# The opening of a convolution-and-expansion kernel rebuilt: taps spread by PE, bands from bf16 products, idle matmuls, w_in in column halves, unit 0 ahead of tile 0, channels regrouped in the cast

## Chip, cores, metric

One core of a Trainium2 chip. The metric is the device time of one execution in microseconds (us), the median of several; lower is better. All runs quoted are of state fast. Spans and points in time come from the profiled execution of each kernel, which is some 1.8 us shorter than its device time.

## The reference

```python
# x: 8 x 4096 x 192 fp32; weight: 8 heads x 7 taps; w_in 192 x 2048; w_out 2048 x 192
w = softmax(weight, axis=-1)                    # per head
conv[b, s, head, :] = sum_k w[head, k] * x[b, s + k - 6, head, :]     # zeros before s = 0
h = conv.reshape(32768, 192) @ w_in
out = (h * cos(h)) @ w_out                      # 32768 x 192, fp32
```

## The kernel before

Tokens come in units of 1024 and tiles of 512. The convolution is a matmul: a band matrix per head (`band`, 128 x 256, bf16), built on the chip from the softmaxed taps, is multiplied by x in bf16. The result is copied to SBUF (`ct`), turned by a DMA transpose into `cT`, and tile after tile goes through the expansion (`h`, L264), the cosine on ACT, the product `g` on DVE (L274) and the second matmul (`o_ps`, L290). The steady loop isn't touched by the change; the opening is. Cut to that:

```python
w_bc = consts.tile([128, H, K], FP32)           # taps, to all partitions by one DMA
nc.scalar.dma_start(out=w_bc, in_=bass.AP(... ap=[[0, 128], [K, H], [1, K]]))
load_unit(0, 0, NB)                             # first half of unit 0
w_src = moe_w_in.rearrange("(h k r) (t f) -> k t h r f", h=H, r=R, t=2)
for k in range(NC):                             # w_in: 6 loads
    for t in range(2):
        nc.sync.dma_start(out=w_f[64 * t : 64 * t + 64, k, :, :]..., in_=w_src[k, t])
load_unit(0, NB, UB); load_unit(1)
...                                             # softmax: 5 DVE steps and one exp -> wn
prod = consts.tile([128, H, E, K], FP32)
strip = consts.tile([128, H, E], FP32)
for eng, hs in ((nc.vector, slice(0, 4)), (nc.gpsimd, slice(4, 8))):
    eng.tensor_tensor(out=prod[:, hs], in0=mask..., in1=wn[:, hs]..., op=ALU.mult)
    nc.vector.tensor_reduce(out=strip[:, hs], in_=prod[:, hs], ..., op=ALU.add)
    for q in range(4):
        eng.tensor_copy(out=band[32 * q : 32 * q + 32, hs, 32 * q : 32 * q + E], in_=strip[...])
...
def cast_unit(u, n0=0, n1=UB):
    copy = nc.scalar.copy if u == 0 and n0 == 0 else nc.gpsimd.tensor_copy
    ...
    copy(out=bf[u][:, n0 + 1 : n1 + 1, :], in_=x_tiles[u][:, n0:n1, :])
...                                             # first half of unit 0 convolved and transposed by PE
nc.gpsimd.tensor_copy(out=w[:, 0], in_=w_f[:, 0])
nc.vector.tensor_copy(out=w[:, 1], in_=w_f[:, 1])
nc.scalar.copy(out=w[:, 2], in_=w_f[:, 2])
...
# h: an expansion step; a, b: second half of unit 0; c, d: convolution of unit 1 (tile 0) or later ones;
# m8: 8 steps of the second matmul; s: cosine and product; ea...: copies of a convolution
PE_ORDER = "h0 c1 m8 c2 h1 m8 h2 h3 m16 | h4 h5 m8 h6 m12 h7 m12"
ACT_ORDER = "P s0 ec s1 s2 s3 Q s4 s5 s6 s7"
PE_FIRST = "h0 a1 h1 a2 b1 h2 b2 h3 | h4 h5 d1 h6 d2 c1 h7 c2 x"      # tile 0
ACT_FIRST = "s0 s1 ea s2 eb s3 s4 s5 s6 ed s7 ec"
```

## Time and profile before

| | kernel before |
|---|---|
| device time, median of 4 | 755.99 us (755.06 to 756.5) |
| profiled span | 753.7 us |
| PE busy | 724.6 us, 96% |
| start of the first `g` on DVE | 22.24 us |
| start of tile 1's first expansion step | 34.36 us |
| start of tile 2's first expansion step | 52.08 us |
| from there to the end | 701.6 us |

Once PE is saturated, a change of the opening moves everything after by a constant, so I mark three points and the stretches between them.

### The profile page before, as it was taken

To read this page: it belongs to the slowest core of one execution; us is meant where nothing else is said; L and a number is where in the kernel's file an instruction comes from. 1 tells how busy PE (TensorE), PEld (TensorE's weight loads), DVE (VectorE), ACT (ScalarE), POOL (GpSimd) and SP (SyncE) were. 2 spreads that over 40 slices of the span, in tenths; PEclk is the share of its full clock that TensorE was granted. 3 is DMA by queue.
4 is the path that set the end of the run, shared out by engine and by line. 5 is a ranking of instruction groups with operands and counts; after the bars stand their busy time and mean duration, and the time that the engine had idled before them with its cause. 6 is when DMAs were issued, how large, how long until landed. Compare 5 with 4: busy or idle time off the path is not lost.

```text
span 753.7 us, 26680 instructions
## 1 busy us (share of the span) xinstructions
PE 724.6 (96%) x12060; PEld 646.8 (86%) x12060; DVE 616.5 (82%) x533; ACT 624.4 (83%) x778; POOL 110.0 (15%) x112
## 2 busy tenths in 40 slices
PE   1699999999999999999999999999999999999997
PEld 1378999999999999999999999999999999999876
DVE  5658888888888888888888888888888888888893
ACT  3668888888888888888888888888888888888883
POOL 4310111110111110011111011111101111101000
PEclk9989999999999999999999999999999999999999
DMA  7434334334535424433432442442454543243301
GB/s 203 113 86 127 85 108 127 94 99 127 116 77 127 127 77 116 127 90 103 128 105 88 127 120 73 127 127 74 119 128 89 104 127 107 86 128 85 82 27 64
DMA packets 167633, 79.99 MB, mean 106 GB/s; under 512 B 99552, under 2 KB 167136, under 8 KB 167520
## 3 DMA queue, kind: packets, MB, share of 16 engines
q1 hardware_dynamic: 167376, 78.26, 39.1%
q8 instruction: 94, 1.54, 0.8%
q14 instruction: 19, 0.16, 0.1%
q10 hardware_dynamic: 144, 0.03, 0.0%
HBM read 28.34 MB, written 25.17 MB: 71 GB/s over the span
## 4 chain that ended last, share of the span: by engine, by line
PE 95%; POOL 1%; issue 1%; DVE 1%; ACT 1%; DMA 1%; POOLq 0%; SPq 0%
PE h L264 46%; PE o_ps L290 45%; PE h L168 3%; DMA w_bc<-in_weight_dram 1%; POOL x_bf L157 0%; POOL wo L360 0%; DVE strip L123 0%; DVE band L125 0%; ACT o_sb L302 0%; ACT cs L270 0%; DVE prod L121 0%; POOL band L125 0%; ACT w L250 0%; POOL ct L218 0%; ACT ct L182 0%
## 5 line engine op out<-in xcount | busy, mean ns | idle before, releaser
L274 DVE TENSOR_TENSOR g<-h,cs 128x1024 bf16<-128x1024 f32 x512 | 605.5, 1221 | 115.8 <-ACT cs L270 108.9
L270 ACT ACTIVATE cs<-h 128x1024 bf16<-128x1024 f32 x512 | 511.4, 1025 | 78.9 <-PE h L264 74.3
L290 PE MATMUL o_ps<-wo,g 64*128 64x192 bf16 x8192 | 452.5, 243 | 1.2 <-ACT o_sb L302 1.2
L290 PEld LDWEIGHTS <-g 64*128 64x128 bf16 x8192 | 419.8, 94 | 35.8 <-SPq L138 1.8
L264 PE MATMUL h<-cT,w 64*128 64x512 bf16 x3072 | 439.1, 379 | 2.9 <-ACT ct L182 1.3
L264 PEld LDWEIGHTS <-w 64*128 64x128 bf16 x3072 | 234.1, 94 | 37.9 <-issue 4.1
L218 POOL COPY ct<-ct 128x1536 bf16<-128x1536 bf16 (+1 forms) x32 | 46.4, 1449 | 580.9 <-ACT ct L182 580.9
L168 PE MATMUL h<-x_bf,band 64*128 64x192 bf16 (+2 forms) x784 | 74.7, 247 | 19.7 <-DVE band L125 11.4
L168 PEld LDWEIGHTS <-band 64*128 64x128 bf16 (+1 forms) x784 | 56.2, 96 | 27.6 <-DVE band L125 11.4
L182 ACT CAST ct<-h 128x384 bf16<-128x384 f32 (+1 forms) x128 | 54.4, 477 | 23.9 <-PE h L168 19.2
L302 ACT COPY o_sb<-o_ps 128x384 f32<-128x384 f32 x128 | 61.3, 479 | 10.1 <-PE o_ps L290 8.2
L157 POOL CAST x_bf<-x_f 128x1536 bf16<-128x1536 f32 (+1 forms) x32 | 46.3, 1448 | 3.1 <-DMA x_f<-in_x_dram 3.1
L156 POOL COPY x_bf<-x_bf 128x192 bf16<-128x192 bf16 x24 | 8.4, 349 | 0.0
L180 ACT CAST ct<-h 128x384 bf16<-128x384 f32 x2 | 1.0, 480 | 6.8 <-PE h L168 6.8
L121 POOL TENSOR_TENSOR prod<-mask,wn 128x1064 f32<-128x1064 f32 x1 | 3.4, 3387 | 4.6 <-DVE wn L116 4.6
L180 DVE CAST ct<-h 128x384 bf16<-128x384 f32 x2 | 1.1, 558 | 3.1 <-ACT ct L180 3.1
L109 ACT ACTIVATE wexp<-wexp 128x56 f32<-128x56 f32 x1 | 0.2, 249 | 3.4 <-DVE wexp L108 3.4
L360 POOL CAST wo<-wo_f 128x1536 bf16<-128x1536 f32 x2 | 2.9, 1469 | 0.0
L243 PE MATMUL h<-ident,ct 128*128 128x128 bf16 x12 | 1.5, 312 | 1.2 <-DVE ct L180 1.2
L123 DVE TENSOR_REDUCE strip<-prod 128x152 f32<-128x1064 f32 x2 | 2.5, 1260 | 0.1
L243 PEld LDWEIGHTS <-ct 128*128 128x128 bf16 x12 | 1.2, 144 | 1.4 <-DVE ct L180 1.4
L88 ACT ACT_TABLE_LOAD x1 | 1.3, 1283 | 1.2 <-PEq L394 1.2
(29 smaller groups left out, 18.3 us busy)
## 6 DMA issues: line engine op xcount, KB each, us to landing
out_dram<-o_sb SPq DMA_DIRECT2D x64, 384.0 KB, 2.8
x_f<-in_x_dram SPq DMA_DIRECT2D x31, 768.0 KB, 12.9
w_f<-in_moe_w_in_dram SPq DMA_DIRECT2D x6, 256.0 KB
wo_f<-in_moe_w_out_dram SPq DMA_DIRECT2D x1, 1536.0 KB
x_f<-in_x_dram SPq DMA_DIRECT2D x2, 384.0 KB, 8.9
cT<-ct SPq DMA_TRANSPOSE x32
w_bc<-in_weight_dram ACTq DMA_DIRECT2D x1, 28.0 KB, 4.8
```

Of the source, the lines that this page charges most:

```text
L121: eng.tensor_tensor(out=prod[:, hs], in0=mask.rearrange("p (o e) k -> p o e k", o=1).to_broadcast([128, 4, E, K]), in1=wn[:, hs].to_broadc ...
L156: nc.gpsimd.tensor_copy(out=bf[u][:, 0, :], in_=bf[u - 1][:, UB, :])
L157: copy(out=bf[u][:, n0 + 1 : n1 + 1, :], in_=x_tiles[u][:, n0:n1, :])
L168: return nc.tensor.matmul(out=pv[:, i // 2, i % 2], lhsT=band[rows, h, 128 if prev else 0 : 256 if prev else 128], rhs=bf[u][rows, n0 + 1 ...
L182: copies[b](o[:, :, 0, :], i[:, :, 0, :])
L218: nc.gpsimd.tensor_copy(out=ct[:, n0:n1, :, 1, :], in_=ct[:, n0:n1, :, 0, :])
L264: nc.tensor.matmul(out=h[:, i, :], lhsT=w[rows, k, j, :], rhs=c[rows, n0 : n0 + NB, k, :], start=(k == 0), stop=(k == NC - 1))
L270: nc.scalar.activation(out=cs, in_=h, func=AF.Sin, bias=math.pi / 2.0, scale=1.0)
L274: nc.vector.tensor_tensor(out=g_tiles[t][:, 2 * j : 2 * j + 2, :], in0=h, in1=cs, op=ALU.mult)
L290: m = nc.tensor.matmul(out=o_ps[tt, b][:, si * D : (si + 1) * D], lhsT=g_tiles[tt][rows, f, s * 128 : (s + 1) * 128], rhs=wo[rows, f // 2, ...
L302: nc.scalar.copy(o_sb[t][:, 2 * b : 2 * b + 2, :].rearrange("p s d -> p (s d)"), o_ps.pop((t, b))[:, 0 : 2 * D])
L360: nc.gpsimd.tensor_copy(out=wo[:, :, i, :], in_=wo_f[:, i])
```

## The change

Its intent is to shorten the time to the first tile and to let tiles 0 and 1 run like steady ones: fewer bytes and fewer steps between the taps and the bands, PE kept at full clock by matmuls on zeros, w_in usable by halves, no convolution of unit 0 between the steps of tile 0, and unit 2's convolution late enough in tile 1. The core of it (left out: the second half of unit 0 is loaded ahead of w_in, w_out later and in 4 loads, and a memset that PE waited for moves to POOL's start):

```diff
-    w_bc = consts.tile([128, H, K], FP32)
-    nc.scalar.dma_start(out=w_bc, in_=bass.AP(... ap=[[0, 128], [K, H], [1, K]]))
+    w_row = consts.tile([1, H * K], FP32)
+    nc.scalar.dma_start(out=w_row, in_=weight.rearrange("(o h) k -> o (h k)", o=1))
...
-    w_src = moe_w_in.rearrange("(h k r) (t f) -> k t h r f", h=H, r=R, t=2)      # 6 loads
+    w_src = moe_w_in.rearrange("(m k) (t f) -> t m k f", k=NC, t=2)              # 4 loads, 2 column halves
...
+    keep_warm(3)                      # 128x512 matmuls on zeros
+    nc.tensor.matmul(out=w_all[:, 0 : H * K], lhsT=one[0:1, :], rhs=w_row, start=True, stop=True)
+    keep_warm(16)
...
-    prod, strip: fp32, half the heads on DVE, half on POOL, tensor_reduce on DVE
+    prod = consts.tile([128, H, E, KP], BF16)
+    for hs in (slice(0, 4), slice(4, 8)):
+        nc.vector.tensor_tensor(out=prod[:, hs], in0=mask..., in1=wn[:, hs]..., op=ALU.mult)
+        for m in (4, 2):
+            nc.vector.tensor_tensor(out=prod[:, hs, :, 0:m], in0=prod[:, hs, :, 0:m], in1=prod[:, hs, :, m : 2 * m], op=ALU.add)
+        for q in range(4):            # the last add writes the band
+            nc.vector.tensor_tensor(out=band[p, hs, ...], in0=prod[p, hs, :, 0], in1=prod[p, hs, :, 1], op=ALU.add)
...
-        copy(out=bf[u][:, n0 + 1 : n1 + 1, :], in_=x_tiles[u][:, n0:n1, :])
+        copy(out=bf[u][...].rearrange("p n (h k r) -> p (n h) k r", h=H, k=NC),
+             in_=x_tiles[u][...].rearrange("p n (h r k) -> p (n h) k r", h=H, k=NC))
...
+    # all of unit 0 convolved ahead of tile 0, then w's first column half cast
-    PE_FIRST = "h0 a1 h1 a2 b1 h2 b2 h3 | h4 h5 d1 h6 d2 c1 h7 c2 x"
-    ACT_FIRST = "s0 s1 ea s2 eb s3 s4 s5 s6 ed s7 ec"
+    PE_FIRST = ["h0 h1 h2 h3 h4 h5 h6 d1 h7 d2 c1 c2 |", "h0 m8 h1 m8 h2 h3 m16 | h4 c1 h5 m8 c2 h6 m12 h7 m12"]
+    ACT_FIRST = ["s0 s1 s2 s3 s4 s5 s6 ed s7 ec", "s0 s1 s2 s3 s4 s5 ec s6 s7"]
```

More of the change, by code (lines that the diff above doesn't have):

```diff
@@ L58 @@
     ctx.enter_context(tc.manual_schedule())
-    w_bc = consts.tile([128, H, K], FP32)
-    nc.scalar.dma_start(out=w_bc, in_=bass.AP(tensor=weight.tensor, offset=weight.offset, ap=[[0, 128], [K, H], [1, K]]))
+    w_row = consts.tile([1, H * K], FP32)
+    nc.scalar.dma_start(out=w_row, in_=weight.rearrange("(o h) k -> o (h k)", o=1))
     x_tiles = {}
@@ L72 @@
     load_unit(0, 0, NB)
+    load_unit(0, NB, UB)
     w_f = consts.tile([128, NC, NP, 128], FP32)
-    w_src = moe_w_in.rearrange("(h k r) (t f) -> k t h r f", h=H, r=R, t=2)
-    for k in range(NC):
+    w_src = moe_w_in.rearrange("(m k) (t f) -> t m k f", k=NC, t=2)
+    HP = NP // 2
+    for q in range(2):
         for t in range(2):
-            nc.sync.dma_start(out=w_f[64 * t : 64 * t + 64, k, :, :].rearrange("p j f -> p (j f)"), in_=w_src[k, t])
-    load_unit(0, NB, UB)
+            nc.sync.dma_start(out=w_f[64 * t : 64 * t + 64, :, q * HP : (q + 1) * HP, :].rearrange("p k j f -> p k (j f)"),
+                              in_=w_src[t, :, :, q * HP * 128 : (q + 1) * HP * 128])
@@ L80 @@
     load_unit(1)
-    wo_f = consts.tile([128, 2, NP, D], FP32)
-    nc.sync.dma_start(out=wo_f, in_=moe_w_out.rearrange("(i j p) d -> p i j d", i=2, p=128))
-    one = consts.tile([128, 1], FP32)
+    wo_f = consts.tile([128, NP, 2, D], FP32)
+    wo_src = moe_w_out.rearrange("(i j p) d -> p j i d", i=2, p=128)
+    one = consts.tile([128, 128], FP32)
     nc.vector.memset(one, 1.0)
-    scrap = consts.tile([128, 1], FP32)
-    nc.scalar.activation(out=scrap, in_=one, func=AF.Exp)
-    E = 32 + K - 1
@@ L92, with keep_warm @@
-    mask = consts.tile([128, E, K], FP32)
+    zero = consts.tile([128, T], BF16)
+    nc.vector.memset(zero, 0.0)
+    idle = o_pools[0].tile([128, T], FP32, name="o_ps0")
+    def keep_warm(n):
+        for _ in range(n):
+            nc.tensor.matmul(out=idle, lhsT=zero[:, 0:128], rhs=zero, start=True, stop=True)
+    scrap = consts.tile([128, 1], FP32)
+    nc.scalar.activation(out=scrap, in_=one[:, 0:1], func=AF.Exp)
+    keep_warm(3)
+    w_all = o_pools[1].tile([128, T], FP32, name="o_ps1")
@@ L93 @@
+    w_bc = w_all[:, 0 : H * K].rearrange("p (h k) -> p h k", k=K)
+    nc.tensor.matmul(out=w_all[:, 0 : H * K], lhsT=one[0:1, :], rhs=w_row, start=True, stop=True)
+    keep_warm(16)
+    xb0 = xbf_pool.tile([128, UB + 1, D], BF16, name="x_bf")
+    nc.gpsimd.memset(xb0[:, 0, :], 0.0)
+    E, KP = 32 + K - 1, 8
+    mask = consts.tile([128, E, KP], BF16)
     nc.gpsimd.memset(mask[0:32], 0.0)
     nc.gpsimd.affine_select(out=mask[0:32], in_=mask[0:32], compare_op=ALU.not_equal, fill=1.0, base=1 - K,
-                            pattern=[[1, E], [1, K]], channel_multiplier=-1)
+                            pattern=[[1, E], [1, KP]], channel_multiplier=-1)
@@ L96 @@
+    for q in range(1, 4):
+        nc.gpsimd.tensor_copy(out=mask[32 * q : 32 * q + 32], in_=mask[0:32])
     ident = consts.tile([128, 128], BF16)
@@ L99 @@
                             channel_multiplier=-1)
-    for q in range(1, 4):
-        nc.vector.tensor_copy(out=mask[32 * q : 32 * q + 32], in_=mask[0:32])
+    wn = consts.tile([128, H, 1, KP], BF16)
+    nc.vector.memset(wn, 0.0)
     band = consts.tile([128, H, 256], BF16)
@@ L109 @@
     nc.scalar.activation(out=wexp, in_=wexp, func=AF.Exp)
-    nc.scalar.activation(out=scrap, in_=one, func=AF.Sin)
+    nc.scalar.activation(out=scrap, in_=one[:, 0:1], func=AF.Sin)
     wsum = consts.tile([128, H, 1], FP32)
@@ L114 @@
     nc.vector.reciprocal(winv, wsum)
-    wn = consts.tile([128, H, 1, K], FP32)
-    nc.vector.tensor_tensor(out=wn[:, :, 0, :], in0=wexp, in1=winv.to_broadcast([128, H, K]), op=ALU.mult)
-    prod = consts.tile([128, H, E, K], FP32)
-    strip = consts.tile([128, H, E], FP32)
-    for eng, hs in ((nc.vector, slice(0, 4)), (nc.gpsimd, slice(4, 8))):
-        eng.tensor_tensor(out=prod[:, hs], in0=mask.rearrange("p (o e) k -> p o e k", o=1).to_broadcast([128, 4, E, K]),
-                          in1=wn[:, hs].to_broadcast([128, 4, E, K]), op=ALU.mult)
-        nc.vector.tensor_reduce(out=strip[:, hs], in_=prod[:, hs], axis=mybir.AxisListType.X, op=ALU.add)
+    nc.vector.tensor_tensor(out=wn[:, :, 0, 0:K], in0=wexp, in1=winv.to_broadcast([128, H, K]), op=ALU.mult)
+    prod = consts.tile([128, H, E, KP], BF16)
+    for hs in (slice(0, 4), slice(4, 8)):
+        nc.vector.tensor_tensor(out=prod[:, hs], in0=mask.rearrange("p (o e) k -> p o e k", o=1).to_broadcast([128, 4, E, KP]),
+                                in1=wn[:, hs].to_broadcast([128, 4, E, KP]), op=ALU.mult)
+        for m in (4, 2):
+            nc.vector.tensor_tensor(out=prod[:, hs, :, 0:m], in0=prod[:, hs, :, 0:m], in1=prod[:, hs, :, m : 2 * m], op=ALU.add)
         for q in range(4):
-            eng.tensor_copy(out=band[32 * q : 32 * q + 32, hs, 32 * q : 32 * q + E], in_=strip[32 * q : 32 * q + 32, hs])
+            p = slice(32 * q, 32 * q + 32)
+            nc.vector.tensor_tensor(out=band[p, hs, 32 * q : 32 * q + E], in0=prod[p, hs, :, 0], in1=prod[p, hs, :, 1], op=ALU.add)
     w = consts.tile([128, NC, NP, 128], BF16)
@@ L150, in cast_unit @@
         copy = nc.scalar.copy if u == 0 and n0 == 0 else nc.gpsimd.tensor_copy
-        if n0 == 0:
+        if u == 0:
+            bf[u] = xb0
+        else:
             bf[u] = xbf_pool.tile([128, UB + 1, D], BF16, name="x_bf")
@@ L156, in cast_unit @@
                 nc.gpsimd.tensor_copy(out=bf[u][:, 0, :], in_=bf[u - 1][:, UB, :])
-        copy(out=bf[u][:, n0 + 1 : n1 + 1, :], in_=x_tiles[u][:, n0:n1, :])
+        copy(out=bf[u][:, n0 + 1 : n1 + 1, :].rearrange("p n (h k r) -> p (n h) k r", h=H, k=NC),
+             in_=x_tiles[u][:, n0:n1, :].rearrange("p n (h r k) -> p (n h) k r", h=H, k=NC))
         bf.pop(u - 2, None)
@@ L229, with conv_first, turn_first @@
     cast_unit(0, 0, NB)
+    cast_unit(0, NB, UB)
     ct_tiles[0] = ct_pool.tile([128, UB, NC, 2, 64], BF16, name="ct")
-    for c in range(2):
-        ps = h_pool.tile([128, 2, T], FP32, name="h")
-        for i in range(4):
-            for prev in range(2):
-                conv_mm(0, c, conv_view(ps, NB), i, slice(0, 128), prev, 0, NB, start=prev == 0 and i % 2 == 0, stop=prev == 1)
-        conv_out(0, c, ps, 0, NB, [nc.scalar.copy, nc.vector.tensor_copy], double=True)
-    cast_unit(0, NB, UB)
-    cT[0] = cT_pool.tile([128, UB, NC, 128], BF16, name="cT")
-    for half in range(2):
+    cT[0] = cT_pool.tile([128, UB, NC, 128], BF16, name="cT")
+    copies = [nc.scalar.copy, nc.vector.tensor_copy]
+    def conv_first(n0, n1):
+        for c in range(2):
+            ps = h_pool.tile([128, 2, T], FP32, name="h")
+            for i in range(4):
+                for prev in range(2):
+                    conv_mm(0, c, conv_view(ps, NB), i, slice(0, 128), prev, n0, n1,
+                            start=prev == 0 and i % 2 == 0, stop=prev == 1)
+            yield
+            conv_out(0, c, ps, n0, n1, copies, double=n0 == 0)
+    def turn_first(half):
         ps = h_pool.tile([128, 2, T], FP32, name="h")
@@ L245 @@
                                  start=True, stop=True, skip_group_check=True)
-        copy = nc.vector.tensor_copy if half else nc.scalar.copy
-        copy(out=cT[0][:, 2 * half : 2 * half + 2].rearrange("p n c k -> p n (c k)"), in_=ps[:, :, 0 : NC * 128])
-    nc.gpsimd.tensor_copy(out=w[:, 0], in_=w_f[:, 0])
-    nc.vector.tensor_copy(out=w[:, 1], in_=w_f[:, 1])
-    nc.scalar.copy(out=w[:, 2], in_=w_f[:, 2])
+        yield
+        copies[half](out=cT[0][:, 2 * half : 2 * half + 2].rearrange("p n c k -> p n (c k)"), in_=ps[:, :, 0 : NC * 128])
+    list(conv_first(0, NB))
+    b = conv_first(NB, UB)
+    next(b)
+    next(b)
+    across = [turn_first(0), turn_first(1)]
+    next(across[0])
+    list(b)
+    for half in range(2):
+        list(across[half])
+    cast = [nc.gpsimd.tensor_copy, nc.vector.tensor_copy, nc.scalar.copy]
+    for k in range(NC):
+        cast[k](out=w[:, k, 0:HP], in_=w_f[:, k, 0:HP])
+    double_unit(0, NB, UB)
+    turn_unit(0, NB, UB)
+    for q in range(2):
+        for i in range(2):
+            nc.sync.dma_start(out=wo_f[:, q * HP : (q + 1) * HP, i], in_=wo_src[:, q * HP : (q + 1) * HP, i])
+    nc.gpsimd.tensor_copy(out=w[:, :, HP:NP], in_=w_f[:, :, HP:NP])
+    cast_unit(1)
+    for q in range(2):
+        nc.gpsimd.tensor_copy(out=wo[:, q * HP : (q + 1) * HP], in_=wo_f[:, q * HP : (q + 1) * HP])
+    load_unit(2)
     g_tiles = {}
@@ L321 @@
         if t == 0:
-            conv.update(a=conv_part(0, 0, NB, UB), b=conv_part(0, 1, NB, UB), d=conv_part(1, 0))
-        act, done, h, step = (ACT_ORDER if t else ACT_FIRST).split(), set(), {}, 0
+            conv["d"] = conv_part(1, 0)
+        act, done, h, step = (ACT_ORDER if t > 1 else ACT_FIRST[t]).split(), set(), {}, 0
         def flush():
@@ L342 @@
         flush()
-        for k in (PE_ORDER if t else PE_FIRST).split():
+        for k in (PE_ORDER if t > 1 else PE_FIRST[t]).split():
             if k[0] == "h" and t < NT:
@@ L353 @@
             flush()
-            if t == 0:
-                if k == "h3":
-                    double_unit(0, NB, UB)
-                    cast_unit(1)
-                    for i in range(2):
-                        nc.gpsimd.tensor_copy(out=wo[:, :, i, :], in_=wo_f[:, i])
-                if k == "|":
-                    turn_unit(0, NB, UB)
-                    load_unit(2)
-                if k == "x":
-                    double_unit(1)
-                    turn_unit(1)
-                    cast_unit(2)
-                continue
+            if k == ("|" if t == 0 else "h1") and second == 0 and cu < NU:
+                double_unit(cu)
             if k == "|":
@@ L377 @@
                     cast_unit(u + 2)
-            if k == "h1" and second == 0 and cu < NU:
-                double_unit(cu)
 _INS = ['x', 'weight', 'moe_w_in', 'moe_w_out']
```

## The prediction

> **What bounds the kernel now.** I read four views in this order: the page's 40 slices, the table of stretches, the chain that ended last, and the timeline of the first 52 us. The slices say where there is anything to gain.
>
> ```profile
> PE   1699999999999999999999999999999999999997
> PEclk9989999999999999999999999999999999999999
> PE 95%; POOL 1%; issue 1%; DVE 1%; ACT 1%; DMA 1%; POOLq 0%; SPq 0%
> ```
>
> From slice 3 (about 50 us) to the end, PE is saturated. The change touches only work before that, so it can win only there. To size it I cut the opening where tile 0's first expansion matmul starts (19.6), where tile 1's does (34.4) and where tile 2's does (52.08). The last row is tile 2, as a yardstick.
>
> ```profile
> core 0: us, PE busy (x) PEld busy (x) DVE busy (x) ACT busy (x) POOL busy (x), PEclk, DMA share, GB/s
> 0.00:19.60 19.60, 3.08 (x28) 2.50 (x29) 10.57 (x21) 6.65 (x10) 8.60 (x16) 1.00 0.73 209
> 19.60:34.40 14.80, 11.63 (x96) 5.54 (x98) 8.84 (x8) 8.57 (x13) 5.36 (x5) 1.00 0.50 125
> 34.40:52.08 17.68, 13.55 (x163) 10.49 (x158) 9.29 (x8) 10.22 (x13) 3.17 (x3) 0.81 0.35 89
> 52.08:62.65 10.57, 10.57 (x181) 8.54 (x178) 8.99 (x9) 9.20 (x13) 3.17 (x3) 1.00 0.34 79
> ```
>
> A steady tile costs 10.57 us; tile 0 took 14.80, tile 1 17.68, and 19.6 us passed ahead of both. Everything after 52.08 (753.7 - 52.08 = 701.6 us of the profiled span) keeps its order of instructions on PE, ACT and DVE. The chain names the parts of the opening.
>
> ```profile
> 0.74 4.85 DMA w_bc<-in_weight_dram
> 7.12 1.28 DVE prod L121
> 8.43 1.27 DVE strip L123
> 9.72 0.93 DVE band L125
> 11.42 1.27 DVE strip L123
> 14.17 0.27 POOL x_bf L154
> 14.48 1.37 PE h L168 x15
> ```
>
> The reader sees the taps land at 5.6, the softmax end at 7.1, the band matrix built until 14.1 by DVE and POOL in turn, and PE let go only by a 0.27 us memset queued behind it. The timeline has the second stall.
>
> ```profile
> 28.38 1.47 POOL L157 CAST x_bf<-x_f 128x1536 bf16<-128x1536 f32 x1
> 29.79 2.88 POOL L360 CAST wo<-wo_f 128x1536 bf16<-128x1536 f32 x2
> 36.25 1.47 POOL L218 COPY ct<-ct 128x1536 bf16<-128x1536 bf16 x1 [3.58 <-ACT ct L182]
> 37.95 1.47 POOL L157 CAST x_bf<-x_f 128x1536 bf16<-128x1536 f32 x1
> 39.47 0.50 PE L168 MATMUL h<-x_bf,band 64*128 64x192 bf16 x4 [4.12 <-POOL x_bf L157]
> ```
>
> Tile 1 puts unit 2's convolution right after its first expansion step, and this waits 4.12 us for POOL's cast of unit 2. From 39.5 to 45 us PE then ran at half clock (0.53 granted), which is another 2.7 us lost.
>
> **What the Trainium skill says.** "TensorE: Matmul & The Clock Gate", Part 1: PE runs at 1.2 GHz until it has been busy for a window of about 3.4 us, then at 2.4, and falls back after an idle window. The trace agrees: expansion matmuls started from 19.6 to 26.7 have a median of 631 ns, those from 44.7 on 376 ns, and the 4.12 us stall is followed by a half clock. "VectorE: DVE Perf Modes", the tier table: a bf16 tensor_tensor in SBUF gets 2 elements a cycle, fp32 and tensor_reduce one; the same page gives (N + 151)/0.96 ns for the fp32 form. For N = 1064 that is 1.27 us, exactly what prod took. "GPSIMD Engine Reference", Performance pitfalls: a read with a step over 8 bytes costs about 2.9 instead of 1.9 cycles per element. The new cast reads fp32 at step 3, 12 bytes. No run before has such a read.
>
> **The change part by part.**
>
> *Taps.* The broadcast load of 28 KB (4.85 us) becomes one row of 224 bytes, spread over partitions by a ones matmul. The median store of 384 KB lands 2.8 us after issue, so I put the row at 0.74 + 2.6 = 3.3, and the product in PSUM at 3.9 (estimate: 0.5 for an fp32 matmul on a cold PE). The softmax is the same five DVE steps and one exp, 1.5 us (5.61 to 7.10 before): taps ready at 5.4 instead of 7.1. The gain is 1.7.
>
> *Bands.* Per half: the product has 4 x 38 x 8 = 1216 bf16 elements, (608 + 151)/0.96 = 0.79; the adds of 608 and 304 elements 0.47 and 0.32; the four band adds of 152, read at a step, so one per cycle, 4 x 0.32 = 1.28; with gaps 3.0. Two halves on DVE alone end at 5.4 + 6.1 = 11.5; at one element a cycle it would be 13.7. Before it was 14.1, plus the memset to 14.44, which moves to POOL's start. The head half can start PE at 8.5, when x is cast (table load of the sine ends about 6.2, the x load at about 6.6, cast 0.81: 7.4).
>
> *Unit 0 ahead of tile 0.* PE: second half of the bands 11.5 to 12.2; unit 0's second half adds 16 matmuls, 1.3 us, ahead of the PE transposes; they end about 14.9. Copies of 0.80 (ACT) and 0.96 (DVE) follow to 15.9, then DVE's cast of its third of w in half the size, 0.4. Tile 0 starts at 16.0 instead of 19.6: 3.6 gained of the about 6 by which the first convolution is earlier (14.48 to 8.5), the rest going to the second half's work and DVE's queue. w_in: x (0.79 MB) and the first column half (0.79 MB), at the 1.08 MB that had moved by 8 us and some 200 GB/s after, are in by about 10.5, cast by 12: beside the path.
>
> *Tile 0.* No second matmul lies in it, so DVE's product g at 1.22 us sets the pace: expansion ends at 16.9, cos 1.02, first g out at 19.2, the seventh at 26.5. Three buffers for h: unit 1's convolution has to take two of them between the last steps, its copies (2 x 0.43 each, in ACT's order ahead of the last cos) end at 27.5, and then tile 1 starts, 11.5 us after tile 0, instead of 14.8: 3.3 gained, by the convolution of unit 0 that has gone and the warm PE.
>
> *Tile 1.* Its convolution stands after the fifth step instead of the first, and second matmuls come first, unpaired, as only tile 0 exists, so each costs what a pair does later: 14 of them took 1.31 us from 45.59 before, 0.09 each. The last g of tile 0 leaves at 29.7, so step h1 waits for its buffer until then; after that PE follows with 7 expansion steps at 0.65, m24 unpaired 2.2, the convolution 0.9 and 32 pairs 2.7: 10.4, and some waits on g of 0.8. That is 40.9 instead of 52.08. So the tile takes 13.4 instead of 17.7: 4.3 gained, the stall and the half clock. POOL's cast of unit 2 follows the doubling of unit 1 (29.4 to 30.8) and ends at 32.7 to 35, while it is needed at 34.4. It just fits.
>
> Sum: 3.6 + 3.3 + 4.3 = 11.2 us off 756.4: 745.2.
>
> *Beside the path.* wo in 4 loads, cast by about 26.5 and needed from 28.3 (first half) and 32.5. The transposes of unit 1 are issued about 31 and need some 5 us, which is due at 40.9. The regrouping cast on POOL, at worst 1536 x 2.9/1.2 = 3.7 us (estimate from the GPSIMD page) instead of 1.47, has some 5 us between its usual end at 58.35 and the convolution at 63.8 in the steady part. That adds nothing to the 30 later units.
>
> **The rivals.**
>
> *Only the waits move.* Tile 0 and 1 are bound by DVE (16 products at 1.22 are 19.5 us), so what is won ahead of tile 0 stays won, but warmth of PE within them is worth little. Against it: up to 45 us DVE waited 8 times, 13.2 us in all, for cos, so before it was not yet the bound. If the bands run at one element a cycle or the taps land late, the first tile starts at 18: gain 8 to 9, time 747 to 748.
>
> *The cast by regrouping becomes a bound.* If POOL's cast costs over 6.5 us, each unit of 21 us stalls PE and the time goes over 770; a cast of 4 to 5 us would only make unit 2's convolution late, 1 to 2 us in all (746 to 747). Against the first: one engine's read at a step has to cost over four times more, and the page says half more.
>
> *The opening goes better than I have it.* PE warm at the transposes and no wait for the last copies (ACT is idle while DVE builds bands) would start tile 0 at about 14.5 and tile 2 at 38: 742 to 743. For it: I have chained each buffer and each copy in full. A gain of 15 us, which over 2% takes, needs tile 2 at 37: only 10 us after tile 1's start, below a steady tile.
>
> **Range and chances.** The centre is the sum, 745.2. Terms that can go wrong are the bands (2 us), landing of the taps (1), the two tiles' waits (2) and the POOL cast (2), mostly independent, so about 3 us either way: 742 to 749. Within 2% means 741.5 or more and up to 771.5. Faster by over 2% needs every term to go well: 0.07. Slower needs the steady part to break: 0.02.
>
> **What would show each step.** In the changed profile the taps' wait should end about 3.3, the product on DVE should take 0.8 (right) or 1.4 (wrong), tile 0's first 64x512 matmul should start at 16 with a duration of 0.38 and not 0.63, tile 1's at 27.5 and tile 2's at 41, with no half clock between 36 and 45. The cast by POOL should take 1.5 to 3.7, and PE after tile 2 should be 9 in each slice with 10.57 us a tile. A tile 2 that starts at 41 with an end not 11 us earlier, or a POOL wait ahead of each convolution, would make the prediction wrong.

## The result

| | before | changed |
|---|---|---|
| device time, median of 4 | 755.99 us | 746.10 us (745.58 to 746.35) |
| ratio | | 0.987 (0.9853 to 0.9887) |
| profiled span | 753.7 | 744.1 |
| start to first `g` | 22.24 | 20.55 |
| first `g` to tile 1 | 12.12 | 9.35 |
| tile 1 | 17.72 | 12.29 |
| tile 2 to the end | 701.6 | 701.9 |

The forecast was 745.2, with 742 to 749 as its range. The kernel is 1.3% faster; the prediction gave a gain of over 2% a chance of 0.07.

The three stretches gave 1.7, 2.8 and 5.4 us, and 0.3 is lost after. First the slices of the changed kernel, which differ from before in the first two places (37 us) and hardly elsewhere, and then the engines' shares of the chain that ended last.

```profile
PE   5899999999999999999999999999999999999997
PE 96%; DVE 3%; ACT 1%; issue 0%; DVEq 0%
```

POOL and the taps' DMA have gone from the chain, and DVE has 3% in place of 1%. The table of stretches (length, then busy time and number of instructions of PE, PEld, DVE, ACT and POOL, granted clock of PE, share and rate of the DMA), cut at the first expansion matmul of tiles 0, 1 and 2:

```profile
0.00:17.65 17.65, 10.50 (x65) 5.81 (x66) 13.24 (x29) 7.27 (x12) 6.80 (x16) 0.90 0.76 178
17.65:29.90 12.25, 9.52 (x73) 3.87 (x74) 9.35 (x8) 7.96 (x10) 6.49 (x5) 0.86 0.81 226
29.90:42.19 12.29, 11.50 (x158) 8.47 (x157) 9.56 (x8) 10.11 (x13) 3.99 (x3) 1.00 0.58 129
```

A steady tile takes 11.11 us in both kernels, from first expansion step to first expansion step (mean of tiles 4 to 61; tile 3 starts at 63.16 before and at 53.24 now). The 10.57 that the prediction calls a steady tile is only the width of the window that it chose, 52.08 to 62.65, which ends ahead of tile 3. Tile 1 now runs at full clock throughout (1.00; 0.81 before). But the clock of the first two stretches is below one. (Before, this column shows 1.00 in the first two stretches, although expansion matmuls of 631 ns lie in the second: the kernel's first record of the clock comes at 27.6 us, and the column counts what lies ahead of it as full. There the durations decide.) The chain in order of time (start, length, what) has the reason and the terms of the opening.

```profile
1.33 1.46 PE o_ps L95 x3
2.79 0.62 PE o_ps L102 x2
...
5.03 0.80 DVE prod L140
5.85 0.49 DVE prod L143
6.36 1.39 DVE prod L143
7.77 0.42 DVE band L146
...
11.14 0.44 DVE prod L143
...
13.36 2.10 PE h L193 x24
...
17.54 1.27 DVE w L291
```

The product takes 0.80 as worked out. The add of 304 elements takes 1.39 us in the first half and 0.44 in the second. The eight band adds take 0.42 each. The second half's convolution starts at 13.36, after PE had nothing to do for 3.3 us, and its 24 matmuls take 2.10 us, at half clock (0.50 granted from 12.7 to 16.0); then tile 0 waits for a cast of w by DVE. And in tile 1 (timeline: start, length, engine, line, operation):

```profile
33.30 2.28 POOL L181 CAST x_bf<-x_f 128x1536 bf16<-128x1536 f32 x1
36.15 0.24 PE L193 MATMUL h<-x_bf,band 64*128 64x192 bf16 x1
```

Unit 2's cast ends at 35.58, and its convolution, now after the fifth expansion step, starts at 36.15 with no wait. Before, PE stood 4.12 us for it.

### The profile page after: what moved, and what is told of

The parts are those of the page before. It is cut to its first block, busy times and chain, and to the rows that moved or that the text cites. A ratio compares the mean times of both kernels' runs of the same rounds, so it can differ in the third digit from the quotient of the medians.

```text
span 744.1 us, 26716 instructions
## 1 busy us (share of the span) xinstructions
PE 727.9 (98%) x12073; PEld 647.4 (87%) x12073; DVE 619.7 (83%) x541; ACT 624.2 (84%) x776; POOL 134.2 (18%) x111
## 4 chain that ended last, share of the span: by engine, by line
PE 96%; DVE 3%; ACT 1%; issue 0%; DVEq 0%
PE h L315 47%; PE o_ps L341 45%; PE h L193 3%; DVE g L325 1%; DVE band L146 0%; DVE prod L143 0%; ACT cs L321 0%; DVE prod L140 0%; ACT ct L207 0%; PE o_ps L95 0%; ACT o_sb L353 0%; DVE w L291 0%; PE h L274 0%; PE o_ps L102 0%; DVE zero L90 0%
## 5 line engine op out<-in xcount | busy, mean ns | idle before, releaser
L193 PE MATMUL h<-x_bf,band 64*128 64x192 bf16 (+1 forms) x776 | 73.0, 244 | 5.1 <-DVE band L146 4.7
L181 POOL CAST x_bf<-x_f 128x1536 bf16<-128x1536 f32 (+1 forms) x32 | 72.4, 2262 | 2.1 <-DMA x_f<-in_x_dram 2.1
L207 ACT CAST ct<-h 128x384 bf16<-128x384 f32 (+1 forms) x126 | 54.0, 480 | 21.3 <-PE h L193 21.3
L193 PEld LDWEIGHTS <-band 64*128 64x128 bf16 (+1 forms) x776 | 55.3, 95 | 11.2 <-DVE band L146 5.3
L95 PE MATMUL o_ps<-zero 128*128 128x512 bf16 x19 | 6.3, 493 | 1.3 <-DVE zero L90 1.3
L95 PEld LDWEIGHTS <-zero 128*128 128x128 bf16 x19 | 2.0, 116 | 4.3 <-issue 1.9
L146 DVE TENSOR_TENSOR band<-prod 32x152 bf16<-32x152 bf16 x8 | 3.3, 417 | 0.1
L143 DVE TENSOR_TENSOR prod<-prod 128x608 bf16<-128x608 bf16 (+1 forms) x4 | 3.0, 760 | 0.1
L177 POOL MEMSET x_bf<- 128x192 bf16 x7 | 1.8, 258 | 0.0
```

Source lines behind the costliest of these rows:

```text
L95: nc.tensor.matmul(out=idle, lhsT=zero[:, 0:128], rhs=zero, start=True, stop=True)
L146: nc.vector.tensor_tensor(out=band[p, hs, 32 * q : 32 * q + E], in0=prod[p, hs, :, 0], in1=prod[p, hs, :, 1], op=ALU.add)
L181: copy(out=bf[u][:, n0 + 1 : n1 + 1, :].rearrange("p n (h k r) -> p (n h) k r", h=H, k=NC), in_=x_tiles[u][:, n0:n1, :].rearrange("p n (h ...
L193: return nc.tensor.matmul(out=pv[:, i // 2, i % 2], lhsT=band[rows, h, 128 if prev else 0 : 256 if prev else 128], rhs=bf[u][rows, n0 + 1 ...
L207: copies[b](o[:, :, 0, :], i[:, :, 0, :])
```

## The experiments

My theory is that one serial path leads from the taps to the first `g`, that a second one of fixed length leads from there to tile 2, and that the gain is the sum of what each part takes off these. The rivals: all of it comes from the new order in tile 1; the warm PE makes it; the gains of the parts hide one another. Each experiment is an edit of the changed kernel. Every kernel gave a correct result. The points in time of each, from its own profile:

| run | device time | ratio to before | span | first `g` | to tile 1 | tile 1 | rest |
|---|---|---|---|---|---|---|---|
| changed kernel | 746.10 | 0.987 | 744.1 | 20.55 | 9.35 | 12.29 | 701.9 |
| after_again (the same) | 745.87 | 0.9863 | 744.6 | 21.06 | 9.34 | 12.30 | 701.9 |
| u1_early_conv | 751.37 | 0.9952 | 749.4 | 20.99 | 9.19 | 17.32 | 701.9 |
| u2_no_warm | 745.40 | 0.9875 | 743.5 | 19.96 | 9.41 | 12.29 | 701.8 |
| u4_taps_dma | 747.97 | 0.9907 | 746.1 | 22.62 | 9.34 | 12.29 | 701.9 |
| u5_unit0_in_tile0 | 749.49 | 0.9927 | 748.4 | 22.14 | 12.13 | 12.29 | 701.8 |
| i1_act_cast | 744.71 | 0.9847 | 742.8 | 19.46 | 9.20 | 12.29 | 701.9 |
| i2_warm_gap | 745.56 | 0.9858 | 743.6 | 20.28 | 9.20 | 12.29 | 701.8 |
| i3_w_early | 745.81 | 0.9860 | 743.9 | 20.35 | 9.34 | 12.29 | 701.9 |
| u3_plain_cast | 745.71 | 0.9864 | 743.8 | 20.18 | 9.48 | 12.29 | 701.9 |
| u6_fp32_bands | 747.35 | 0.9886 | 745.5 | 21.74 | 9.33 | 12.29 | 702.1 |
| c2_combined_strip | 741.52 | 0.9812 | 739.6 | 16.49 | 9.04 | 12.30 | 701.8 |

On three chips: u1, u2, u4, u5; after_again, i1, i2, i3; u3, u6, c2. The intervals of the ratios are some 0.0012 to 0.0018 to either side (about 1 us), so differences of 0.5 us between device times of different calls say nothing. Two profiles of the very same kernel differ by 0.5 us at the first `g`. Only i1, i2 and i3 have an unaltered kernel beside them; the others are compared with it. They were run at other times.

**after_again.** The changed kernel once more.

> The changed kernel unaltered, as the yardstick for the three beside it on the same chip. Ratio to the kernel before 0.987 within 0.002; span within 1 us of 744.1; tile 2 starts at 42.2 within 0.7.

It came as expected but for the start of tile 2, 42.70, at the edge. The 24 convolution matmuls took 2.10 us as in the first profile, but the 12 transposes 1.46 instead of 1.17, since the clock came back later. That is the scatter to keep in mind below.

**u1: tile 1's order put back.**

```diff
-    PE_FIRST = [..., "h0 m8 h1 m8 h2 h3 m16 | h4 c1 h5 m8 c2 h6 m12 h7 m12"]
-    ACT_FIRST = [..., "s0 s1 s2 s3 s4 s5 ec s6 s7"]
+    PE_FIRST = [..., PE_ORDER]
+    ACT_FIRST = [..., ACT_ORDER]
```

> The changed kernel, with tile 1's order of PE and ACT put back to the steady order (unit 2's convolution right after the first expansion step). Theory (the sum of three stretches): POOL's cast of unit 2 ended at 35.6 us in the changed kernel and the convolution would be reached at about 30.7, so PE stands some 4.5 us and then runs part of tile 1 at half clock; time 750 to 752, tile 1 at 16 to 18 us instead of 12.3. Rival (tile 1 is bound by DVE anyway, so the order is worth nothing): within 1 us of 746.1.

Measured: 751.37 us, tile 1 17.32. The timeline of this run:

```profile
33.58 2.23 POOL L181 CAST x_bf<-x_f 128x1536 bf16<-128x1536 f32 x1
35.87 0.50 PE L193 MATMUL h<-x_bf,band 64*128 64x192 bf16 x4 [4.86 <-POOL x_bf L181]
37.70 1.51 PE L315 MATMUL h<-cT,w 64*128 64x512 bf16 x6
```

PE stands 4.86 us for the cast and then runs an expansion step in 1.51 us instead of 0.82. The order alone is worth 5.0 us of tile 1's 5.4, which is half the change's gain. It isn't all of it: even so the kernel is 0.9952 of before. So the rival "all of it is the order" falls, and so does "the order is worth nothing".

**u2: no idle matmuls.**

```diff
-    keep_warm(3)
-    keep_warm(16)
```

> The changed kernel without its 19 idle matmuls on zeros. The trace after shows PE at half clock again from 13.3 to 23 us, so the idle matmuls sped up only the first 8 convolution matmuls (0.51 us against some 0.75), whose successor waits for DVE anyway. Theory from the trace: 746.1, within 0.5. Rival (my prediction's wording: warm PE is part of what tile 0 gained): 747.5 to 749.

Measured: 745.40 us. The first `g` is not later but 0.6 to 1.1 earlier. PE in this run:

```profile
2.08 0.64 PE L101 MATMUL o_ps<-w_row,one 1*128 1x56 f32 x2 [2.08 <-DMA w_row<-in_weight_dram]
8.93 0.82 PE L191 MATMUL h<-x_bf,band 128*128 128x96 bf16 x8 [6.21 <-DVE band L144]
12.76 2.10 PE L191 MATMUL h<-x_bf,band 128*128 128x96 bf16 x24 [3.01 <-DVE band L144]
```

The row of taps is there at 2.08; with three idle matmuls ahead of it the product ran at 2.72. They delay the taps by 0.64 and everything with them. The other 16 make the first eight convolution matmuls 0.51 instead of 0.82 us, which nobody waits for, and by the second half the clock has fallen in both kernels (2.10). The clock is low there for two reasons: in this run it hadn't risen yet (the first eight already took 0.82), in the changed kernel it had fallen. So the idle matmuls of the change gain nothing. That they cost 0.6 is read from the profile alone: every profile with the three idle matmuls has the product at 2.72 or 2.73, both without them at 2.07 or 2.08, while the time is 0.2 under the range expected (746.1 within 0.5) and the ratio, 0.9875, isn't better than the changed kernel's. (The half clock that the expectation reads from 13.3 to 23 was two stretches, 12.7 to 16.0 and 19.5 to 22.8, with 1.00 between.)

**u4: the taps by the broadcast load.**

```diff
-    nc.scalar.dma_start(out=w_row, in_=weight.rearrange("(o h) k -> o (h k)", o=1))
+    nc.scalar.dma_start(out=w_bc, in_=bass.AP(... ap=[[0, 128], [K, H], [1, K]]))
```

> The changed kernel with the taps loaded by the broadcast DMA of 28 KB again, read from SBUF; no product with ones. The first softmax step started at 5.61 with that load and at 3.43 with the product. Theory (one serial chain on DVE from the taps to tile 0): everything up to tile 2 moves by 2 us, 748.0 to 748.5. Rival (a later wait on w_in, x or POOL absorbs it): under 747.

Measured: 747.97 us, the low end of what was expected. The first softmax step started at 5.00 (3.43 in the changed kernel), 1.6 later, and the first `g` 1.6 to 2.1 later. So nothing between absorbs it: the path is serial. The term of the taps is 1.6 to 2.

**u5: unit 0's second half inside tile 0 again.**

```diff
-    list(conv_first(0, NB)); b = conv_first(NB, UB); ...     # both halves ahead
+    list(conv_first(0, NB))
-    PE_FIRST = ["h0 h1 h2 h3 h4 h5 h6 d1 h7 d2 c1 c2 |", ...]
+    PE_FIRST = ["h0 a1 h1 a2 b1 h2 b2 h3 h4 h5 h6 d1 h7 d2 c1 c2 |", ...]
```

> The changed kernel with the second half of unit 0 convolved inside tile 0 again, by half rows, as before the change, instead of ahead of it. Theory: tile 0 starts 1.5 to 2 us earlier (16 matmuls, two pairs of copies less ahead of it), but becomes longer by 2 to 4 us, as the convolution takes h buffers and ACT time between cosines: 746.5 to 748.5. Rival (only moved work): 745 to 746.5.

Measured: 749.49 us (747.85 to 750.48), over the range expected. From the first `g` to tile 1 it takes 12.13, as before the change (12.12), instead of 9.35: the expected 2 to 4. But tile 0 didn't start earlier. The timeline, which is that of the slowest of the six executions:

```profile
17.44 2.23 POOL L181 CAST x_bf<-x_f 128x1536 bf16<-128x1536 f32 x1 [0.37 <-DMA x_f<-in_x_dram]
17.84 2.12 DVE L285 CAST w<-w_f 128x512 bf16<-128x512 f32 x1
20.01 1.04 PE L306 MATMUL h<-cT,w 64*128 64x512 bf16 x4 [1.45 <-DVE w L285]
```

With less work for POOL ahead, its cast of unit 1 fell just beside DVE's cast of w, which took 2.12 us, 1.26 in the changed kernel and 0.43 where no cast of POOL lay beside it (i3). The edit moves more than the convolution: the loads of w_out are issued at 5.5 instead of 18.7, and the clock stays at 0.50 from 12.4 to 29.2, where the changed kernel is at full clock from 22.95. So the run shows what the convolution costs in tile 0 together with this half clock (2.8 us), but not each alone, and not what it costs ahead of tile 0.

**i1: the second cast of unit 0 by ACT.** In the changed kernel the slow add of 304 elements lay beside a cast by POOL:

```profile
5.85 1.89 DVE L143 TENSOR_TENSOR prod<-prod 128x608 bf16<-128x608 bf16 x2
6.22 1.22 POOL L181 CAST x_bf<-x_f 128x768 bf16<-128x768 f32 x1 [2.09 <-DMA x_f<-in_x_dram]
```

```diff
-        copy = nc.scalar.copy if u == 0 and n0 == 0 else nc.gpsimd.tensor_copy
+        copy = nc.scalar.copy if u == 0 else nc.gpsimd.tensor_copy
```

> The changed kernel with the cast of unit 0's second half on ACT instead of POOL. In the trace the add of 304 elements on DVE took 1.38 us while POOL's cast ran (6.22 to 7.44) and 0.43 in the second half, without it. Theory (POOL's cast keeps DVE's two-input instruction waiting): that add takes 0.43, the first half of the bands ends 0.95 earlier, and everything up to tile 2 moves by 0.9: about 0.9 us under the unaltered kernel. Rival (the add is slow in itself, by its short runs): the add stays at 1.4 or the wait is elsewhere; no gain.

Measured: 744.71 us beside 745.87 for the unaltered kernel, so 1.2 us.

```profile
5.86 0.95 DVE L143 TENSOR_TENSOR prod<-prod 128x608 bf16<-128x608 bf16 x2
```

The two adds take 0.95 instead of 1.89: the POOL cast was the cause, and the rival (slow in itself) falls. u2 shows the same from the other side. There DVE was 0.7 us ahead, its two adds took 0.94, and POOL's cast (6.11 to 7.31) fell on the four band adds, which took 2.72 us instead of 1.71. The time gained is a little more than the 0.9 expected; the 24 convolution matmuls also ran faster, 1.49 instead of 2.10.

**i2: idle matmuls in the gap that matters.**

```diff
             conv_out(0, c, ps, n0, n1, copies, double=n0 == 0)
+            if c == 0 and n0 == 0:
+                keep_warm(12)
```

> The changed kernel with 12 more idle matmuls between the two halves of the convolution, where PE stood for 3.3 us and fell to half clock. Theory: 24 convolution matmuls take 1.4 instead of 2.1 us, the transposes 0.85 instead of 1.2, tile 0 starts 0.8 to 1.0 earlier; and if the clock then holds over the wait for w_in, its first matmuls run at 0.38 instead of 0.63: 1.0 to 1.7 us under the unaltered kernel. Rival (DVE and ACT copies set the pace, the clock is hidden): within 0.4.

Measured: 745.56 us, which is 0.3 under the unaltered kernel, not clear of noise, and so the rival's range. The profile:

```profile
13.36 1.20 PE L193 MATMUL h<-x_bf,band 128*128 128x96 bf16 x24 [0.74 <-DVE band L146]
18.15 4.23 PE L317 MATMUL h<-cT,w 64*128 64x512 bf16 x22 [0.73 <-DVE w L293]
```

The 24 matmuls take 1.20 instead of 2.10, as expected. But the next wait, of DVE's cast of w, takes the time up, and the clock falls over it (22 expansion matmuls in 4.23 us). The expectation of 1.0 to 1.7 was too high. Most of the warmth is hidden.

**i3: w cast early.**

```diff
             conv_out(0, c, ps, n0, n1, copies, double=n0 == 0)
+            if c == 0 and n0 == 0:
+                for k in (1, 2):
+                    cast[k](out=w[:, k, 0:HP], in_=w_f[:, k, 0:HP])
```

> The changed kernel with the casts of w_in's first column half by ACT and DVE put between the copies of the first and second convolution part, where both engines stand idle (0.8 and 3.6 us), instead of behind the copies of the transposes. Theory: DVE's cast of 1.26 us (beside a POOL cast) leaves the path; tile 0's first full step starts 1.2 earlier; 1.2 us under the unaltered kernel. Rival (w_in isn't there by then, or another wait takes its place): within 0.4.

Measured: 745.81 us, no gain: a miss. DVE's cast did leave the path (0.43 us at 14.07, in a gap), but:

```profile
13.51 1.19 PE L193 MATMUL h<-x_bf,band 128*128 128x96 bf16 x24 [3.37 <-DVE band L146]
17.79 4.68 PE L317 MATMUL h<-cT,w 64*128 64x512 bf16 x24 [1.14 <-DVE cT L281]
```

Here tile 0 starts at 17.79 with all six matmuls of its first step at half clock (first cosine at 19.29), whereas in the changed kernel four of the six ran warm after the wait (18.85, first cosine 19.50). The half clock took the place of the wait. (In the profile of after_again, whose first step was also at half clock, the first cosine came at 20.00, so single profiles scatter by as much as this gain.) The two have to be removed together, which c2 tries.

**u3: channels not regrouped.**

```diff
-    w_src = moe_w_in.rearrange("(m k) (t f) -> t m k f", k=NC, t=2)          # 4 loads
+    w_src = moe_w_in.rearrange("(h k r) (t f) -> k t h r f", h=H, r=R, t=2)  # 12 loads
-        copy(out=bf[u]....rearrange("p n (h k r) -> p (n h) k r"), in_=x_tiles[u]....rearrange("p n (h r k) -> ..."))
+        copy(out=bf[u][:, n0 + 1 : n1 + 1, :], in_=x_tiles[u][:, n0:n1, :])
```

> The changed kernel with the channels no longer regrouped in the casts: x is cast in order, and w_in is loaded by 12 loads of one channel group each, so that the result is the same. Theory: POOL's cast of a unit takes 1.47 again instead of 2.26 and ACT's 0.81 instead of 1.23; unit 2's cast no longer matters, as it is late by nothing; on DVE's path the wait behind POOL's cast shrinks from 0.95 to some 0.6: 0.2 to 0.6 us under the unaltered kernel (745.3 to 745.9), if the 12 loads, which cost 0.63 of issue each, bring the first half of w_in in time. Rival (the strided loads are the reason for the regrouping): w_in comes 2 us or more later and tile 0 with it, 747 to 749.

Measured: 745.71 us, the same as the changed kernel; the 0.2 to 0.6 expected can't be told from nothing. POOL's cast of a unit took 1.47 us again, and w_in wasn't late for its users, for all the 12 loads:

```profile
8.97 0.61 POOL L291 CAST w<-w_f 128x512 bf16<-128x512 f32 x1 [2.47 <-DMA w_f<-in_moe_w_in_dram]
```

POOL's wait for w_in ends at 8.97, in the changed kernel at 9.84 and 11.09 in two profiles. This isn't quite like for like: here POOL's third needs two of the six loads of the first half, there both of two. The thirds of ACT and DVE were cast at 16.5 and 17.3 and waited for no load; when their loads landed, the trace doesn't say. So the regrouping buys no time on the path, and it costs 0.8 us of POOL in each unit, where POOL has room. It is neutral.

**u6: bands in fp32, on DVE and POOL.** The band lines of the kernel before, in the changed one.

> The changed kernel with the bands built as before the change: fp32 products, half on DVE and half on POOL, reduced on DVE, copied by each. In the trace after, the bands took DVE 8.3 us from the last softmax step to PE's second half (5.03 to 13.31); before it was 7.0 (7.12 to 14.12) on two engines. Theory from the traces: as the steps are the same ones, the second half is ready about 1 us earlier, at 12 to 12.5, but POOL casts x only after its own half, at about 12, so unit 0's second half waits: the whole is within 1 us of 746, that is, the bf16 products gain nothing. Rival (the prediction's term, bf16 saves 0.9 and the queueing behind POOL more): 747.5 to 749.

Measured: 747.35 us. My theory of this run fell; its rival (747.5 to 749) missed by 0.15 but had the sign. The fp32 product, first in the kernel before and then in this run:

```profile
7.12 1.27 DVE L121 TENSOR_TENSOR prod<-mask,wn 128x1064 f32<-128x1064 f32 x1
7.17 3.39 POOL L121 TENSOR_TENSOR prod<-mask,wn 128x1064 f32<-128x1064 f32 x1 [4.58 <-DVE wn L116]
```

```profile
5.00 2.34 POOL L140 TENSOR_TENSOR prod<-mask,wn 128x1064 f32<-128x1064 f32 x1 [0.75 <-DVE wn L134]
5.02 3.44 DVE L140 TENSOR_TENSOR prod<-mask,wn 128x1064 f32<-128x1064 f32 x1
```

Two products of the same size at the same time on DVE and POOL: the one that starts 0.05 or 0.02 us earlier runs at its own speed, and the other ends only 2.2 or 1.1 us after the first has ended, nearly its own full time (2.34 and 1.27 when it runs first). They ran one after the other. Before the change DVE came first by 0.05 us; here POOL does, and DVE's path grows by 2.2 us. So the bands of the change, all on DVE and in bf16, are worth some 1.2 to 1.5 us here. That is less than the 2.2 us of this wait alone, so it isn't shown that the bf16 arithmetic gains anything by itself; a run with fp32 products on DVE alone would be needed.

**c2: what the runs point to, together.** x's second half by ACT (i1), no idle matmuls ahead of the taps' product (u2), idle ones in both gaps (i2) together with the early casts of w (i3), and the last add of the bands done once:

```diff
-            nc.vector.tensor_tensor(out=band[p, hs, ...], in0=prod[p, hs, :, 0], in1=prod[p, hs, :, 1], op=ALU.add)   # x4
+        nc.vector.tensor_tensor(out=strip[:, hs], in0=prod[:, hs, :, 0], in1=prod[:, hs, :, 1], op=ALU.add)           # x1
+            nc.vector.tensor_copy(out=band[p, hs, ...], in_=strip[p, hs])                                              # x4
```

> The changed kernel with what the runs so far point to: unit 0's second half cast on ACT (worth 1.2 by itself), no idle matmuls ahead of the product with ones (0.6), idle matmuls in the two gaps of PE (0.3 to 0.9), w_in's casts early (0.1 to 0.7), and the last add of the bands done once on 128 partitions in 0.42 with four copies of 0.23, instead of four adds of 0.42 (0.33 per half). Theory (one serial path to tile 0's first g, 21.6 us fixed from there to tile 2): first g at 16.5 to 17.5 instead of 20.6 to 21.1, tile 2 at 38 to 39; 742 to 743. Rival (w_in's landing at 9.8 to 11.1 or unit 1's load becomes the bound): 744 to 745.

Measured: 741.52 us (741.35 to 741.96), 0.9812 of before (0.9793 to 0.983), 3.9 to 4.6 us under the changed kernel (by the ratios and by the times). It beats both. Whether it is over 2% faster than before, the interval doesn't say.

```profile
6.15 0.43 DVE L144 TENSOR_TENSOR strip<-prod 128x152 bf16<-128x152 bf16 x1
6.62 0.81 DVE L147 COPY band<-strip 32x152 bf16<-32x152 bf16 x4
14.57 2.12 PE L321 MATMUL h<-cT,w 64*128 64x512 bf16 x18
0.00:14.57 14.57, 11.93 (x79) 6.17 (x79) 11.49 (x31) 8.18 (x13) 4.67 (x14) 1.00 0.89 196
14.57:25.53 10.96, 7.93 (x73) 3.46 (x73) 8.01 (x7) 7.86 (x10) 6.11 (x5) 1.00 1.17 257
```

The clock is 1.00 throughout, tile 0's first 18 matmuls take 2.12 us, and the end of each half of the bands (last add and copies) takes 1.28 us instead of 1.71. The first `g` is 4.1 to 4.6 earlier and everything after it by the same, since from there to tile 2 it is 21.3 us (21.6 in the changed kernel).

**Do the parts add up?** Undone one at a time, they cost 5.3 (order of tile 1), 3.4 (unit 0 in tile 0), 1.9 (taps) and 1.2 (bands) us against 746.10, and the idle matmuls and the regrouping gain nothing. That is 11.8 for a change that gained 9.9, so the gains don't hide one another to any large part, but they don't add up cleanly either: u5 carries the half clock with it. Not undone alone: w_in in column halves and the memset that was moved.

## Why the prediction was right, and where not

The time, 746.1, lies 0.9 from the forecast of 745.2, and the gain, 9.9, is 88% of the 11.2 predicted. Part of the closeness is the starting point: the prediction counted from 756.4, the runs of the result from 755.99; from there its gain would have given 744.8. (2% under 756.4 is 741.3, not 741.5.) Its steps:

- *Nothing after tile 2 changes.* Right: 701.6 us before, 701.8 to 702.1 in all twelve profiles, with a steady tile of 11.11 (not the 10.57 that the prediction read, see above; nothing in its sum rests on it). POOL's cast grew from 1.47 to 2.30 us in every unit and cost nothing, as said.
- *Taps, 1.7.* Right, a little low. The last softmax step ended at 4.92 instead of 5.4 (a gain of 2.2), and u4 gives 1.6 to 2 when it is undone. Two errors lie in it: the row was usable at 2.08 (u2) and not at 3.3, and the change's own idle matmuls, which the prediction left out here, held the product until 2.72. The product took 0.67, estimated at 0.5.
- *Bands, ready at 8.5 and 11.5.* Mis-sized: 9.5 and 13.3. The terms were estimates with the formula that the prediction cites. The product was exact (0.79 predicted, 0.79 measured). The add of 304 elements has 0.43 and not 0.32 us; the band adds have 0.42 and not 0.32, eight times; and the largest term is one that I left out, POOL's casts, which hold DVE up by 0.94 in the first half (shown by i1) and about 0.3 in the second (the add of 608 took 0.77 there, 0.49 in the first half). A hint of it stood in the trace before, where POOL's product took 3.39 us beside one of 1.27 on DVE. Altogether the bands took DVE 8.3 us instead of 6.1, longer than the 7.0 before the change on two engines.
- *Tile 0 at 16.0.* Late by the bands' 1.8: its first two matmuls ran at 17.65 and the rest at 18.85, after DVE's cast of w. I had 0.4 us for that cast; it took 1.26 beside a cast by POOL. The first stretch gained 1.7 at the first `g`.
- *Tile 0 in 11.5, with matmuls at 0.38.* The pace was right: I had the first `g` start 9.5 us ahead of tile 1 (19.2 - 1.22 to 27.5), and it was 9.35, with seven products of DVE back to back from 20.55 to 28.86. That unit 0's convolution, with the half clock that lasted as long, had cost 2.8 of it is shown by u5. The warm PE was wrong. The clock fell while PE stood 3.3 us between the halves of the bands, came back at 16.1 and fell again at 19.5, after waits of 1.14 and 0.81 us for the casts ahead of tile 0; the matmuls from 17.65 to 23.2 have a median of 0.54 us. It didn't matter much, as DVE's pace hides it after the first step: in c2, at full clock, the stretch took 9.04. Ahead of the first `g` it costs 0.3 to 0.8 (i2's first `g` against that of the two unaltered profiles).
- *Tile 1 in 13.4.* Better than that, 12.29. The mechanism (the stall behind POOL's cast and the half clock after it) is shown by u1, at 5.0 us. "It just fits" was right, though both came later than the prediction had them: the cast was done at 35.58 and its first user came at 36.15. One wait was wrong: the second step, h1, did not wait for tile 0's last `g`, which ran from 30.81 to 32.04; it started at 31.58, after 0.22 us for a copy of the convolution by ACT. This gave 0.5 of the 1.1; the rest of the tile took 10.6 instead of the 11.2 reckoned with its waits.

In sum: the first `g` was 2.6 us later than I had it (20.55 against 18.0), the stretch from it to tile 1 0.15 shorter and tile 1 1.1 shorter, so tile 2 came 1.3 late; 0.3 more was lost after it, and the span is 9.6 shorter instead of 11.2. The total is closer than its terms, as two errors went against each other, and that is luck. Of the rivals, "only the waits move" came closest for the opening (it named the bands as what would fail), and "the cast by regrouping becomes a bound" fell: POOL's cast with its read at 12 bytes took 2.30 us beside 1.47 in order (u3), which is 1.56 times, near the "+50%" of "GPSIMD Engine Reference", Performance pitfalls, and it was hidden.

## What to carry to other kernels

Once an engine is saturated, find points that every version has, such as the first product and the first step of tiles 1 and 2, and compare the stretches between; here tile 1 came out equal to 0.01 us in eleven of twelve profiles, and effects of half a us in a stretch could be read that the device time couldn't show (the first product itself scattered by 0.5 us between two profiles of one kernel). Cut a window at the instructions themselves: a width chosen by hand made the "steady tile" 0.5 us too short. Before splitting work between DVE and POOL, look in the trace whether their products or casts lie side by side, as here these ran one after the other (u6, i1); a free ACT was the better second engine (i1). Here idle matmuls helped only where they reached up to the very matmuls that were waited for (c2), and cost time ahead of an instruction that others waited for (u2).

## What the Trainium skill lacked or had wrong

- "GPSIMD Engine Reference", Key points, says that the engine shares its SBUF interfaces with VectorE, with contention for DVE instructions in a 2-port mode or with two SBUF inputs. It gives no size there. That one instruction shuts out the other isn't lacking in the skill: its page on SBUF treats it, which the prediction did not use. The sizes here: 1.27 and 3.39 us with DVE ahead by 0.05 us, 2.34 and 3.44 with POOL ahead by 0.02. A DVE cast of 512 elements took 0.43 alone, 1.26 and 2.12 beside casts by POOL.
- No page was found to have a size for reads at a step on ScalarE: 768 elements took 1.23 us at a step of 12 bytes and 0.82 in order.
- "VectorE: DVE Perf Modes", the tier table, has two elements a cycle for bf16 tensor_tensor. It holds for 1216 elements (0.79 us) and 608 (0.49). The table alone is not enough for short runs (the skill's microarchitecture page on this engine has a rule for them, which the prediction did not use): 304 elements in runs of two took 0.43, where its fp32 formula with two elements a cycle gives 0.32, and 152 elements read at a step of 16 bytes took 0.42 on 32 partitions and 0.43 on 128, where one element a cycle gives 0.32.
- "TensorE: Matmul & The Clock Gate", Part 1, has the fall after an idle window of some 3.4 us that runs free. Nothing is wrong with it, and the sizes are worth knowing: after gaps of 3.31, 3.32 and 3.37 us the same 24 matmuls took 2.10, 1.49 and 1.19 us (changed kernel, i1, i3), as the granted clock fell ahead of them, within them (at 13.2) and only after them (at 14.9).
